# Strassen values for tiles 8 and 9, and a later place for the last two pairs of x, in a linear-attention and MLP kernel

## The chip, the cores and the metric

One core of a Trainium2 chip. The metric is the device time of one execution in microseconds, taken as the median of several runs. A profile comes from one further execution; its span runs from the first to the last instruction.

## What is computed

x is 2048 tokens by 640. Its layer norm feeds a linear attention with a learned feature map (32 heads of 20) and a GELU MLP; the attention's output, times the SiLU of the MLP's output, is added to x. Cut to what matters here:

```python
xn = _layernorm(x, axis=-1)
q, k, v = split(xn @ wqkv)                      # 32 heads of 20 each
pk = einsum("bhsd,hdf->bhsf", k, w_phi)         # pq from q alike
phi_k = concat([softmax(pk), softmax(-pk)])     # phi_q alike
kv = einsum("bhsf,bhsd->bhfd", phi_k, v)
z = einsum("bhsf->bhf", phi_k)
o = (phi_q @ kv) / (phi_q @ z + 1e-6)
s = o @ wo
g = silu(gelu(xn @ w1 + b1) @ w2 + b2)
return x + s * g
```

## The kernel before

Tokens go in 16 tiles of 128. Float32 operands are kept as a high part in the fast matmul type and a low part (value minus high part), and a product is three passes: high x high, high x low, low x high (PASSES).

**Stages.** Keys, queries and values of all tiles come first (about 0 to 238 us of the span); the MLP, and beside it the queries' normalization, follow; then the output product. The change lies in the first stage, between about 95 and 205 us. There the order on every engine is the order in which the code is written.

**A plain projection** (`project`, L392 to L404) multiplies one tile of xn by a 640x640 weight: 5 blocks x 3 passes x 2 halves, 30 matmuls of 320 columns into a `pA` bank. `pA` has three banks, taken in turn. For keys and queries `feat1` (L410 to L425) reads the bank on VectorE (`mx` L413, `e` L416, `nr` L419) and POOL adds the negative half (L420); `feat2` takes the exponential on ScalarE (L429). For keys, `key_fin` sums (L437), takes the reciprocal (L469) on VectorE and scales on POOL (L442). `kv_pair` accumulates keys times values of two tiles on TensorE (L481).

**A Strassen pair** (`token_pair`, L699 to L738) does the projection of two tiles at once with one level of Strassen's product in Winograd's form: seven groups of matmuls (QPARTS: X, Y, X, V, Z, W, Z; L714), 54 instead of 60. It needs sums of blocks of x (`x_sums`, L288; split to `xd` by `t_split`, L307 to L317) and of weights (`value_forms`, L671, split at L648 and L652). ScalarE copies X and Y (`qx`, L718, L720), POOL adds them (`qu`, L721), VectorE adds V (L725) and forms the halves (L728, L731, L735). The last group reads the bank that L728 has read. Hooks run other work between the groups. Before, values of tiles 10 to 15 and queries of tiles 8 to 15 are Strassen pairs; pair q is tiles 2q and 2q+1.

**x for a pair** comes transposed from DRAM (`load_xr`). `pair_stats` takes mean and variance of a tile's rows on VectorE (bn_stats L220), the power -0.5 on POOL (L223), and sends them through DRAM to come back spread over all partitions (`bc`, L326, L328). `pair_sub` (POOL, L335) and `pair_mul` (VectorE, L340) normalize; `plain` writes high parts (ScalarE, L272) and low parts (VectorE, L274); `x_sums` and `t_split` follow.

**The loop around the change** (L762 to L815) goes over tiles 6 to 9: key projection, features, value projection (L458 copies it), key finish, two query projections (`queries`), and between them the x work of pair t - 3. The second loop (L823 to L876) takes p = 5, 6, 7: keys of tiles 2p and 2p+1, kv of the pair before, and the value pair p with its hooks.

## Time and profile before

| | us |
|---|---|
| median of 3 runs (lowest, highest) | 639.72 (638.86, 640.79) |
| the profiled execution | 639.93 |
| its span | 638.2 |
| VectorE busy | 510.5 |
| POOL (GpSimd) busy | 432.9 |
| ScalarE busy | 260.5 |

PE is TensorE's matmuls, PEld its weight loads, DVE VectorE, ACT ScalarE, SP the engine whose queue issues most DMAs. A row of the timeline gives start, length, engine, line, operation, output and inputs; an arrow in brackets names what ended the engine's idle time ahead of it. A row of the chain gives start, length and what held the end at that time.

### The profile page before, as it was taken

The page shows a single profiled execution, that of the slowest core. Times are in us where ns is not written, and L with a number is a line of the kernel's source. Part 1 is how long each engine was busy: PE and PEld are TensorE (multiplying, and loading weights), DVE is VectorE, ACT ScalarE, POOL GpSimd, SP SyncE. Part 2 cuts the span into 40 slices and gives each one's busy share as a digit, 9 for nine tenths or more (in the row PEclk, how much of TensorE's full clock was granted, in tenths as well). Part 3 has the DMA queues.
Part 4 walks back from the last instruction along what each step waited for, and adds up shares of the span by engine and source line. Part 5 has one row for each costly group of instructions (what it writes and reads, how often), then busy time and mean ns, then how long its engine had stood idle before and what let it go on. Part 6 is the DMA issues. An engine that isn't in the chain of part 4 may idle for free.

```text
span 638.2 us, 11443 instructions
## 1 busy us (share of the span) xinstructions
PE 633.0 (99%) x4330; PEld 552.0 (86%) x4330; DVE 510.5 (80%) x784; ACT 260.5 (41%) x389; POOL 432.9 (68%) x377
## 2 busy tenths in 40 slices
PE   9999999999999999999999999999999999999997
PEld 9999999999999998888888888888888888667676
DVE  5886976789788777878989869758798899887585
ACT  3622422334344257243442534842322335455540
POOL 1877466897977764987878776381735678857363
PEclk9999999999999999999999999999999999999999
DMA  8477287394411387449899699797498598969926
GB/s 346 121 234 226 70 286 222 93 299 148 157 43 45 135 273 274 141 95 357 213 280 317 162 368 346 154 318 257 143 238 171 168 187 264 305 184 322 346 71 198
DMA packets 167167, 136.89 MB, mean 214 GB/s; under 512 B 89864, under 2 KB 130824, under 8 KB 166728
## 3 DMA queue, kind: packets, MB, share of 16 engines
q1 hardware_dynamic: 164376, 124.56, 66.0%
q10 hardware_dynamic: 2736, 11.60, 4.8%
q8 instruction: 34, 0.56, 0.4%
q14 instruction: 21, 0.17, 0.1%
HBM read 87.76 MB, written 48.38 MB: 213 GB/s over the span
## 4 chain that ended last, share of the span: by engine, by line
PE 97%; DMA 2%; DVE 0%; SPq 0%; issue 0%; DVEq 0%
PE pB L988 26%; PE pA L401 24%; PE pB L959 23%; PE pB L1190 8%; PE pA L714 6%; PE pB L1116 2%; PE pA L164 2%; PE kv L481 2%; PE qV L714 1%; DMA phT<-phi_t 1%; PE qY L714 1%; DMA xres<-in_xt_dram 1%; PE pA L545 1%; PE pB L1098 0%; PE pA L387 0%; DVE y L1199 0%
## 5 line engine op out<-in xcount | busy, mean ns | idle before, releaser
L988 PE MATMUL pB<-hs,w2s 128*128 128x512 f32 x720 | 165.9, 389 | 0.0
L988 PEld LDWEIGHTS pB<-hs,w2s 128*128 128x128 f32 x720 | 135.0, 188 | 28.8 <-issue 0.8
L959 PE MATMUL pB<-xp,w1s 128*128 128x512 f32 x324 | 81.4, 389 | 0.0
L959 PE MATMUL pB<-xd,w1s 128*128 128x512 f32 x324 | 79.3, 389 | 0.0
L442 POOL TENSOR_TENSOR eq<-eq,rc 128x1280 f32<-128x1280 f32 x16 | 37.9, 2369 | 57.3 <-DVE rc L1050 40.1
L959 PEld LDWEIGHTS pB<-xp,w1s 128*128 128x128 f32 x324 | 60.7, 188 | 12.8 <-ACT x L975 0.3
L959 PEld LDWEIGHTS pB<-xd,w1s 128*128 128x128 f32 x324 | 60.8, 188 | 12.7
L997 DVE TENSOR_TENSOR y<-pB,y 128x512 f32<-128x512 f32 x100 | 63.1, 676 | 1.8 <-PE pB L988 1.8
L964 ACT ACTIVATE pB<-pB,b1t 128x512 f32<-128x512 f32 x48 | 31.8, 662 | 77.4 <-DVE pB L1387 28.9
L429 ACT ACTIVATE e<-e 128x1280 f32<-128x1280 f32 x32 | 40.7, 1273 | 50.1 <-POOL e L420 50.1
L401 PE MATMUL pA<-wk,xp 128*128 128x320 f32 x384 | 59.6, 310 | 0.0
L401 PEld LDWEIGHTS pA<-wk,xp 128*128 128x128 f32 x384 | 56.9, 188 | 0.1
L420 POOL TENSOR_TENSOR e<-nr,e 128x640 f32<-128x640 f32 x32 | 44.7, 1396 | 17.2 <-DVE nr L419 17.2
L1037 POOL TENSOR_TENSOR ez<-eq,zrep 128x1280 f32<-128x1280 f32 x16 | 47.4, 2963 | 6.5 <-DMA eq<-e_dram 6.5
L442 POOL TENSOR_TENSOR e<-e,rc 128x1280 f32<-128x1280 f32 x16 | 37.8, 2367 | 20.4 <-DVE rc L469 20.4
L401 PE MATMUL pA<-wv,xp 128*128 128x320 f32 x240 | 37.0, 310 | 0.0
L509 POOL TENSOR_TENSOR w1s<-raw,w1s 128x640 fp32r<-128x640 f32 (+1 forms) x18 | 25.4, 1412 | 16.0 <-ACT w1s L508 15.9
L139 POOL TENSOR_TENSOR w2s<-raw,w2s 128x640 fp32r<-128x640 f32 x23 | 36.1, 1592 | 0.2 <-ACT w2s L137 0.2
L401 PEld LDWEIGHTS pA<-wv,xp 128*128 128x128 f32 x240 | 35.5, 188 | 0.1
L970 DVE TENSOR_TENSOR hs<-pB,hs 128x512 fp32r<-128x512 f32 x48 | 32.0, 684 | 4.2 <-ACT hs L966 3.8
L137 ACT ACTIVATE w2s<-raw 128x640 fp32r<-128x640 f32 x24 | 17.2, 736 | 43.1 <-DMA xd_dram<-xhi 16.4
L413 DVE TENSOR_REDUCE mx<-pA 128x32 f32<-128x640 f32 x32 | 25.9, 809 | 10.1 <-PE pA L401 9.8
(219 smaller groups left out, 1269.7 us busy)
## 6 DMA issues: line engine op xcount, KB each, us to landing
raw<-in_w_dram SPq DMA_DIRECT2D x42, 320.0 KB, 5.1
e_dram<-e ACTq DMA_DIRECT2D x16, 640.0 KB, 3.9
eq<-e_dram SPq DMA_DIRECT2D x16, 640.0 KB, 5.8
phi_t<-eq SPq DMA_DIRECT2D x64, 160.0 KB, 3.3
phT<-phi_t SPq DMA_DIRECT2D x20, 512.0 KB, 7.5
xt<-in_x_dram SPq DMA_DIRECT2D x16, 320.0 KB, 6.2
xres<-in_xt_dram SPq DMA_DIRECT2D x20, 256.0 KB, 6.7
out_dram<-xres SPq DMA_DIRECT2D x19, 256.0 KB, 4.2
```

The lines of the kernel that those rows point to most:

```text
L139: eng.tensor_tensor(sl[:, 1, :], raw, sl[:, 0, :].bitcast(F32), op=OP.subtract)
L401: nc.tensor.matmul(ps[:, hf, :HALF], stat_x(q, o, k, a), ws[k][:, b, hf * HALF:(hf + 1) * HALF], start=n == 0, stop=n == 3 * KC - 1)
L420: rest = lambda: nc.gpsimd.tensor_tensor(e5[:, :, :, 1, :], nr[:, :, :, None].to_broadcast([P, 2, 16, DH]), e5[:, :, :, 0, :], op=OP.subtract)
L429: nc.scalar.activation(ef, ef, AF.Exp)
L442: nc.gpsimd.tensor_tensor(e3, e3, rc[:, :, None].to_broadcast([P, 64, DH]), op=OP.mult)
L714: nc.tensor.matmul(bank[ch], q_x(blk, a, q), p_weight(base, f, w, k)[:, b], start=ch not in seen and n == 0, stop=n == len(mms) - 1, skip_ ...
L959: nc.tensor.matmul(bank[ch][:], tl[:, a, off + wo_:off + wo_ + P], mov(blk, b), start=new and n == 0, stop=n == len(mms) - 1, skip_group_c ...
L970: nc.vector.tensor_tensor(hs[:, 1], ps, hs[:, 0].bitcast(F32), op=OP.subtract)
L988: nc.tensor.matmul(ps[:], ws[i][:, b, d * P:(d + 1) * P], hs[o][i][:, a, :], start=i == n == 0, stop=(i, n) == (GF - 1, 2), skip_group_che ...
L997: nc.vector.tensor_tensor(y, ps[:], y, op=OP.add)
L1037: nc.gpsimd.tensor_tensor(zv, ef, zf, op=OP.mult)
L1190: nc.tensor.matmul(ps[:, mv], w, o[:, mv], start=first and n == 0, stop=last and n == len(steps) - 1, skip_group_check=True)
```

## The change

The loop over tiles 6 to 9 no longer projects the values of tiles 8 and 9. In the second loop, at p = 5, a value pair 4 stands behind the keys of tiles 10 and 11 and ahead of value pair 5, with the kv block of tiles 8 and 9 behind it; its weight sums are still split in the loop over tile 9 and in pair 4's hooks. The x work of pair 6 moves with it: `pair_sub`, `pair_mul`, `plain`, `x_sums` and `t_split` go from the loop over tile 9 into pairs 4 and 5, and `t_split` gets an engine for its second low part (VectorE for pair 6). The statistics of tiles 14 and 15 move from the loop over tile 8 into pair 4, the loads of their rows from tile 7 to tile 9, the load of pair 7 of x into pair 5. In pair 6 the kv block of tiles 10 and 11 stands behind the first group, and pair 7's high and low parts are written at two places.

```diff
--- before.py
+++ after.py
@@ -304,17 +304,13 @@
         x_sums(lambda a, b: xr[:, a:b, :P], lambda a, b: xr[:, a:b, P:],
                lambda t: xt_two(xr.rearrange("p k (o t) -> p (k o) t", o=2), t))
 
-    def t_split(q, later=False):
+    def t_split(q, eng=nc.gpsimd):
         dst = xd()[:, :, :, at(q)]
         tt = xrs.pop(q).rearrange("p k (o t) -> p (k o) t", o=2)[:, :9]
         nc.scalar.activation(dst[:, :, 0, :], tt, AF.Copy)
 
-        def lo(o):
-            nc.gpsimd.tensor_tensor(dst[:, o, 1, :], tt[:, o], dst[:, o, 0, :].bitcast(F32), op=OP.subtract)
-        lo(slice(0, 5))
-        if later:
-            return lambda: lo(slice(5, 9))
-        lo(slice(5, 9))
+        for o, e in ((slice(0, 5), nc.gpsimd), (slice(5, 9), eng)):
+            e.tensor_tensor(dst[:, o, 1, :], tt[:, o], dst[:, o, 0, :].bitcast(F32), op=OP.subtract)
 
     def pair_stats(t):
         if t % 2 == 0:
@@ -755,8 +751,8 @@
     wq_f, wq_b, wv_f = [], [], []
     queries_done = list(range(NT // 2))
     queries = iter(range(NT // 2))
-    XIN = {6: (12, 13), 7: (14, 15)}
-    STATS = {6: (10, 11), 7: (12, 13), 8: (14, 15)}
+    XIN = {6: (12, 13), 9: (14, 15)}
+    STATS = {6: (10, 11), 7: (12, 13)}
     x_in(10)
     x_in(11)
     for t in range(6, 10):
@@ -767,34 +763,36 @@
             spill(3)
         if t == 9:
             vb = value_forms(sv_raw, [nc.vector, nc.vector, nc.gpsimd, nc.gpsimd])
-            next(vb)
             w_dump(0)
             w_dump(1)
         if t == 6:
             next(vf[1])
         es[t] = feat1(pk)
-        if t == 9:
-            next(vb)
         if t > 6:
             feat2(es[t])
-            pair_mul(q)
-            pair_plain(q)
-            t_sums(q)
+            if t < 9:
+                pair_mul(q)
+                pair_plain(q)
+                t_sums(q)
         else:
             pair_sub(4)
             fold_w(wqT, range(4, KC), "wq", wq_s)
             feat2(es[t])
-        vs[t] = value(t)
-        phis[t] = key_fin(es.pop(t))
+        if t < 8:
+            vs[t] = value(t)
+        if t < 9:
+            phis[t] = key_fin(es.pop(t))
         pq = project(next(queries), wq_s)
         ef = feat1(pq)
-        if t > 6:
-            split_rest = t_split(q, t == 9)
-            if t < 9:
-                load_xr(q + 1)
+        if t == 9:
+            phis[t] = key_fin(es.pop(t))
+        if 6 < t < 9:
+            t_split(q)
+            load_xr(q + 1)
         if t == 8:
             sv_raw = [load_raw(sv_dram[k]) for k in range(4)]
         if t == 9:
+            next(vb)
             next(vb)
         for u in STATS.get(t, ()):
             pair_stats(u)
@@ -804,22 +802,34 @@
         if t == 6:
             next(vf[1])
         if t == 9:
-            next(vb)
-            next(vb)
-            next(vb)
-            split_rest()
-            load_xr(7)
-        if t in (7, 8):
-            pair_sub(q + 1)
+            for _ in range(4):
+                next(vb)
+        if t == 7:
+            pair_sub(5)
         if t < 9:
             store_e(queries_done.pop(0), ef)
-        else:
-            feat2(ef)
         if t == 6:
             kv_pair(4)
         for u in XIN.get(t, ()):
             x_in(u)
     qf, later, last_sums = None, [], []
+
+    def x_last():
+        t_split(6, nc.vector)
+        load_xr(7)
+
+    def first_store():
+        feat2(ef)
+        next(vb)
+
+    def last_stats():
+        nc.scalar.dma_start(e_dram[_tok(queries_done.pop(0))], ef)
+        pair_stats(14)
+
+    def x_mid():
+        pair_mul(6)
+        pair_stats(15)
+
     for p in range(5, 8):
         t = 2 * p
         pk = project(t, wk_s)
@@ -828,14 +838,15 @@
             qf = forms(sq_dram, wq_f, wq_b, [nc.vector, nc.vector, nc.vector, nc.gpsimd])
             next(qf)
         es[t] = feat1(pk)
+        pk = project(t + 1, wk_s)
+        if p > 6:
+            kv_pair(t - 2)
+        es[t + 1] = feat1(pk, later)
+        if p == 5:
+            value_pair(4, {1: first_store, 2: lambda: next(vb, None), 3: lambda: pair_sub(6), 4: last_stats, 6: x_mid})
+            kv_pair(8)
         if p == 6:
             pair_mul(7)
-        pk = project(t + 1, wk_s)
-        kv_pair(t - 2)
-        es[t + 1] = feat1(pk, later)
-        if p == 6:
-            plain(7, 0, xrs[7][:, :, :P])
-            plain(7, 1, xrs[7][:, :, P:], slice(0, 1))
         if p == 7:
             next(qf)
             next(qf)
@@ -845,20 +856,29 @@
 
         def rest(t=t, p=p):
             if p == 5:
-                nc.scalar.dma_start(e_dram[_tok(queries_done.pop(0))], ef)
-                next(vb)
-                next(vb, None)
+                pair_plain(6)
             later.pop(0)()
+            if p == 5:
+                t_sums(6)
+            if p == 7:
+                next(qf)
+
+        def copied(t=t, p=p):
+            feat2(es[t])
             if p == 6:
+                for o in range(2):
+                    plain(7, o, xrs[7][:, :, o * P:(o + 1) * P], lo=False)
+            if p == 7:
+                next(qf)
+
+        def x_next(p=p):
+            if p == 5:
+                x_last()
+            if p == 6:
+                plain(7, 0, xrs[7][:, :, :P], hi=False)
+                plain(7, 1, xrs[7][:, :, P:], slice(0, 1), hi=False)
                 plain(7, 1, xrs[7][:, :, P:], slice(1, 2), False, True)
                 t_sums(7)
-            if p == 7:
-                next(qf)
-
-        def copied(t=t, p=p):
-            feat2(es[t])
-            if p == 7:
-                next(qf)
 
         def first_key(t=t, p=p):
             phis[t] = key_fin(es.pop(t))
@@ -870,10 +890,12 @@
             else:
                 phis[t + 1] = es.pop(t + 1)
                 last_sums.append(key_sums(phis[t + 1]))
+            if p == 5:
+                pair_sub(7)
             if p == 6:
                 t_split(7)
 
-        value_pair(p, {0: lambda: p == 6 and plain(7, 1, xrs[7][:, :, P:], slice(1, 2), True, False), 1: rest, 2: copied, 3: lambda: p == 5 and pair_sub(7), 4: first_key, 6: second_key})
+        value_pair(p, {0: lambda: p == 6 and kv_pair(10), 1: rest, 2: copied, 4: x_next, 5: first_key, 6: second_key})
     w1f = w1_forms(w1r)
 
     def early_rest(q, ea):
```

On TensorE, in the loop over tile 9 (wk are the key weights, wv the value weights, wq the query weights, b blocks of x kept apart) stood before, from the key projection of tile 9 on:

```order
L401 MATMUL pA<-wk_185,b_1381 128x320 x6
L401 MATMUL pA<-wk_196,b_1381 128x320 x6
L401 MATMUL pA<-wk_206,xp 128x320 x6
L401 MATMUL pA<-wk_216,xp 128x320 x6
L401 MATMUL pA<-wk_240,xp 128x320 x6
L401 MATMUL pA<-wv,b_1381 128x320 x12
L401 MATMUL pA<-wv,xp 128x320 x18
L401 MATMUL pA<-wq_854,xp 128x320 x6
```

and now, at the same place:

```order
L397 MATMUL pA<-wk_185,b_1381 128x320 x6
L397 MATMUL pA<-wk_196,b_1381 128x320 x6
L397 MATMUL pA<-wk_206,xp 128x320 x6
L397 MATMUL pA<-wk_216,xp 128x320 x6
L397 MATMUL pA<-wk_240,xp 128x320 x6
L397 MATMUL pA<-wq_854,xp 128x320 x6
L397 MATMUL pA<-wq_1045,xp 128x320 x6
```

The two value rows are gone, and the query projection follows the key projection directly; the same goes for tile 8.

On VectorE, from the features of key tile 11 through pair 5, stood before (qV is the bank of group V, v the value rows, rc the sums of a key tile):

```order
L413 TENSOR_REDUCE mx<-pA 128x32
L416 TENSOR_TENSOR e<-pA,mx 128x32x20
L419 TENSOR_REDUCE nr<-e 128x32
L725 TENSOR_TENSOR qu<-qu,qV 128x320
L728 TENSOR_TENSOR v<-qu,pA 128x16x20
L437 TENSOR_REDUCE rc<-e 128x64
L469 RECIPROCAL rc<-rc 128x64
L731 TENSOR_TENSOR v<-qu,pA 128x16x20
L735 TENSOR_TENSOR v<-qu,pA 128x16x20
```

and now pair 5 stands behind the x work of pair 6:

```order
L336 TENSOR_TENSOR xr<-xr,bc 128x1280
L220 BN_STATS st<-xt 128x6 x2
L221 BN_AGGR st<-st 128x2
L222 TENSOR_SCALAR pst<-st 128x1
L225 COPY pst<-st 128x1
L274 TENSOR_TENSOR xp<-xr,xp 128x5x128
L274 TENSOR_TENSOR b_2157<-xr,b_2157 128x2x128
L274 TENSOR_TENSOR xp<-xr,xp 128x3x128
L721 TENSOR_TENSOR qu<-qu,qV 128x320
L724 TENSOR_TENSOR v<-qu,pA 128x16x20
```

The multiplication (L336), the statistics of tile 15 and three low parts (L274) of pair 6 now stand in front of pair 5's additions.

On POOL, from the sum qx of pair 5 to that of key tile 12's negative half, stood before:

```order
L721 TENSOR_TENSOR qu<-qx 128x320
L652 TENSOR_TENSOR ws<-raw,ws 128x320 x2
L420 TENSOR_TENSOR e<-nr,e 128x32x20
L335 TENSOR_TENSOR xr<-xr,bc 128x5x128 x2
L442 TENSOR_TENSOR e<-e,rc 128x1280 x2
L420 TENSOR_TENSOR e<-nr,e 128x32x20
```

and now:

```order
L717 TENSOR_TENSOR qu<-qx 128x320
L416 TENSOR_TENSOR e<-nr,e 128x32x20
L289 TENSOR_TENSOR xr<-xr 128x2x128 x4
L289 TENSOR_TENSOR xr<-xr 128x128
L313 TENSOR_TENSOR xd<-xr,xd 128x5x128
L438 TENSOR_TENSOR e<-e,rc 128x1280 x2
L331 TENSOR_TENSOR xr<-xr,bc 128x5x128 x2
L416 TENSOR_TENSOR e<-nr,e 128x32x20
```

x_sums of pair 6 (L289) and the first low part of its sums (L313) have come in between, and the mean of pair 7 (L331) stands behind the scaling of keys 10 and 11 (L438) instead of ahead of it.

More of the change, by code (lines that the diff above doesn't have):

```diff
@@ L847, in rest @@
             if p == 5:
-                nc.scalar.dma_start(e_dram[_tok(queries_done.pop(0))], ef)
-                next(vb)
-                next(vb, None)
+                pair_plain(6)
             later.pop(0)()
-            if p == 6:
-                plain(7, 1, xrs[7][:, :, P:], slice(1, 2), False, True)
-                t_sums(7)
+            if p == 5:
+                t_sums(6)
             if p == 7:
@@ L859, in copied @@
             feat2(es[t])
+            if p == 6:
+                for o in range(2):
+                    plain(7, o, xrs[7][:, :, o * P:(o + 1) * P], lo=False)
             if p == 7:
                 next(qf)
+        def x_next(p=p):
+            if p == 5:
+                x_last()
+            if p == 6:
+                plain(7, 0, xrs[7][:, :, :P], hi=False)
+                plain(7, 1, xrs[7][:, :, P:], slice(0, 1), hi=False)
+                plain(7, 1, xrs[7][:, :, P:], slice(1, 2), False, True)
+                t_sums(7)
         def first_key(t=t, p=p):
```

## The prediction

> **What bounds the kernel now.** I read the busy shares first, then who owns the chain that ended last, then that chain in order of time around the edited loop.
>
> ```profile
> PE 633.0 (99%) x4330; PEld 552.0 (86%) x4330; DVE 510.5 (80%) x784; ACT 260.5 (41%) x389; POOL 432.9 (68%) x377
> ...
> PE 97%; DMA 2%; DVE 0%; SPq 0%; issue 0%; DVEq 0%
> ```
>
> ```profile
> 119.55 39.80 PE pA L401 x270
> 159.34 1.32 PE kv L481 x125
> 160.67 1.07 PE pA L714 x6
> ...
> 168.78 8.80 PE pA L401 x60
> ```
>
> TensorE is busy for 633.0 of 638.2 us and owns 97% of the chain. The chain's pieces touch: 119.55 + 39.80 is where the kv block starts (to 0.01), 159.34 + 1.32 where pair 5 starts, and so on to the end of the loop. TensorE waits for nobody here. An edit can win only the matmuls that it takes off, and it loses every wait that it puts on TensorE; the other engines matter where they become late. One 320-column matmul costs 8.80/60 = 0.147 us, a projection of 30 costs 4.40. Pair 5 takes 168.78 - 160.67 = 8.11 us for 54 matmuls, 7.92 at that rate; its first six take 1.07 instead of 0.88, so a break in the stream costs another 0.19. I call the seven groups of a pair parts 1 to 7 (6, 6, 9, 9, 6, 9, 9 matmuls).
>
> **Term 1, the matmuls.** Values of tiles 8 and 9 were 2 x 30 matmuls and are now one pair of 54. Six less at 0.147 us: **-0.88 us**. There are as many kv blocks as before, so the breaks behind them neither grow nor fall. Nothing else leaves TensorE, so this is also the most that can be won.
>
> **Term 2, the bank of query tile 4.** Without the two value projections, query tile 6 comes to stand where key tile 9 stood, at 132.78:
>
> ```profile
> 121.29 3.15 POOL L335 TENSOR_TENSOR xr<-xr,bc 128x640 f32<-128x640 f32 x2
> 124.40 1.27 POOL L420 TENSOR_TENSOR e<-nr,e 128x640 f32<-128x640 f32 x1
> 124.47 2.55 DVE L340 TENSOR_TENSOR xr<-xr,bc 128x1280 f32<-128x1280 f32 x1 [2.60 <-POOL xr L335]
> 127.83 0.83 DVE L274 TENSOR_TENSOR xp<-xr,xp 128x640 fp32r<-128x640 f32 x1 [0.81 <-ACT xp L272]
> 129.93 1.48 DVE L437 TENSOR_REDUCE rc<-e 128x64 f32<-128x1280 f32 x1
> 131.91 0.76 DVE L413 TENSOR_REDUCE mx<-pA 128x32 f32<-128x640 f32 x1
> 132.71 0.82 DVE L416 TENSOR_TENSOR e<-pA,mx 128x640 f32<-128x640 f32 x1
> 132.78 1.92 PE L401 MATMUL pA<-wk,b 128*128 128x320 f32 x12
> ```
>
> A projection takes one of three pA banks in turn, here that of query tile 4, which VectorE frees with the subtraction L416 at 132.71 + 0.82 = 133.53. In front of that stand, unmoved by the change, POOL's subtraction for pair 5 (to 124.44), the multiplication behind it, the low parts of x and the sums of key tile 8, and none is shorter in the new order. Due at 132.78, free at 133.53: 0.75 us, and a break of 0.19 makes **+0.95** (0.75 to 1.0). A value projection of 4.40 us covered it so far. The times below go by the old clock and include this shift.
>
> **Term 3, last part of pair 5.** VectorE and POOL hold each other up when both work on SBUF operands:
>
> ```profile
> 199.64 0.96 POOL L721 TENSOR_TENSOR qu<-qx 128x320 f32<-128x320 f32 x1 [1.88 <-ACT qx L720]
> 199.95 1.01 DVE L652 TENSOR_TENSOR wqb<-raw,wqb 128x320 fp32r<-128x320 f32 x1
> 200.57 1.52 POOL L420 TENSOR_TENSOR e<-nr,e 128x640 f32<-128x640 f32 x1
> 200.88 1.56 DVE L652 TENSOR_TENSOR ws<-raw,ws 128x320 fp32r<-128x320 f32 x1
> ```
>
> They take turns. POOL's instruction ends at 200.60, VectorE's, issued in between, at 200.96; POOL's next ends at 202.09, VectorE's next at 202.44. Each VectorE subtraction of 320 columns needs some 0.36 us of its own and the rest is waiting. The Trainium skill (SBUF — State Buffer, section Who interferes with whom) calls it an exclusive lock that the first to issue holds for its whole instruction; the trace agrees (1.01 and 1.56 us for 0.36). It leaves open who is next when both have more to do. Were it always VectorE, this term would be 0.2 to 0.4, but POOL's chain in term 4 would start as late as it does now and take the difference, so the sum would move by less than 0.2.
>
> The prices:
>
> ```profile
> 103.18 1.48 DVE L340 TENSOR_TENSOR xr<-xr,bc 128x1280 f32<-128x1280 f32 x1
> 128.57 0.42 DVE L274 TENSOR_TENSOR b<-xr,b 128x256 fp32r<-128x256 f32 x1
> L274 DVE TENSOR_TENSOR xp<-xr,xp x12: 544/825/1105, 32.0 to 181.3; 128x384 fp32r<-128x384 f32 x6, 128x640 fp32r<-128x640 f32 x6
> 134.30 0.88 DVE L220 BATCH_NORM_STATS2 st<-xt 128x6 f32<-128x320 f32 x2
> 135.59 0.88 DVE L220 BATCH_NORM_STATS2 st<-xt 128x6 f32<-128x320 f32 x2
> 164.79 0.87 POOL L721 TENSOR_TENSOR qu<-qx 128x320 f32<-128x320 f32 x1
> 165.63 1.72 POOL L652 TENSOR_TENSOR ws<-raw,ws 128x320 fp32r<-128x320 f32 x2
> 165.69 0.49 DVE L725 TENSOR_TENSOR qu<-qu,qV 128x320 f32<-128x320 f32 x1 [1.24 <-POOL qu L721]
> 168.20 0.55 DVE L469 RECIPROCAL rc<-rc 128x64 f32<-128x64 f32 x1
> 185.23 3.61 POOL L289 TENSOR_TENSOR xr<-xr 128x256 f32<-128x256 f32 x5
> 188.80 4.70 POOL L442 TENSOR_TENSOR e<-e,rc 128x1280 f32<-128x1280 f32 x2
> 193.45 2.83 POOL L313 TENSOR_TENSOR xd<-xr,xd 128x640 fp32r<-128x640 f32 x2
> 188.88 1.17 ACT L310 ACTIVATE xd<-xr 128x1152 fp32r<-128x1152 f32 x1 [3.29 <-POOL xr L289]
> ```
>
> The new pair 4 I cost at nothing. It starts at 151.3; its last part, due 6.6 us later at 157.9, reads the odd half that VectorE adds in 0.49 behind part 5 (156.6), at about 157.2. But what follows is late. POOL ended the two weight subtractions (1.72) of pair 5 at 167.35 before, 6.7 us after the pair's start; in pair 4 less stands in front of them, and I take 157.0. Then come POOL's mean of pair 6 (3.15, to 160.2), VectorE's multiplication (1.48, about 161.8) and its statistics of tile 15 (135.59 - 134.30 = 1.29, about 163.1). POOL's power for them (0.5), four memsets (0.3) and the sum of the two qx of pair 5 (L721) wait in that order, so qx starts at about 164.2. At 163.8 the three low parts of x of pair 6 begin on VectorE (0.83, 0.42, 0.54 at the least). In turns: low part to 164.7, qx to 165.5, low part to 165.9, POOL's L420 of key tile 11 (1.27) to 167.1, low part to 167.6, qu + qV and the odd half (0.49 each, 0.1 between) to 168.6. Part 7 of pair 5, due at 167.4, reads that bank: **+1.45** with the break. Without turns the low parts end at 165.5 and the term is 0; if qx is first, it is 2.1.
>
> **Term 4, last part of pair 6.** From there POOL and VectorE form one chain: x_sums (3.61, its first piece free before the third low part ends; 171.0), ScalarE's high part 1.17 (172.2), VectorE's low part of four blocks 0.68 and a value half 0.49, sums and reciprocal of key 10 (1.48 + 0.55, 175.3), value half, the same of key 11 (177.7), POOL's scaling of key 11 (2.35, 180.1), its mean of pair 7 (3.15, 183.2), L420 of key 12 (1.27, 184.5), VectorE's multiplication (1.48, 186.0), qx (0.87, 186.9), two additions (188.0). The four-block low part is new on VectorE: between three blocks (0.54) and five (0.83) I take 0.68, with up to 1.6 more if POOL's five-block half goes first. Moving the kv block of keys 10 and 11 behind part 1 covers the scaling, not this. TensorE comes to part 7 of pair 6 at 185.54 - 0.88 + 0.95 + 1.45 = 187.1: **+1.1** with the break (0 to 2.5).
>
> ```profile
> 185.54 1.04 PE L714 MATMUL pA<-ws,xp 128*128 128x320 f32 x6
> 197.13 1.07 PE pA L714 x6
> ...
> core 0: us, PE busy (x) PEld busy (x) DVE busy (x) ACT busy (x) POOL busy (x), PEclk, DMA share, GB/s
> ...
> 177.00:197.00 20.00, 20.00 (x374) 19.56 (x373) 15.26 (x19) 7.75 (x11) 16.18 (x18) 1.00 0.24 67
> ...
> 196.24 1.27 POOL L420 TENSOR_TENSOR e<-nr,e 128x640 f32<-128x640 f32 x1
> 202.94 0.49 DVE L728 TENSOR_TENSOR v<-qu,pA 128x320 f32<-128x320 f32 x1
> 203.76 1.04 PE L714 MATMUL pA<-ws,xp 128*128 128x320 f32 x6
> ```
>
> The window of pairs 6 and 7 says the same in sums: POOL had 20.0 - 16.18 = 3.8 us idle there, and x_sums and mean of pair 6 bring 6.8 into this stretch while a low part (1.3) leaves.
>
> **Term 5, pair 7.** POOL's backlog (one L420, a low part, sums, two scalings, two low parts behind qx) now ends about 1.4 us after the pair starts; before, it ended at 196.24, 0.9 ahead of the pair's start at 197.13. So the L420 of keys 14 and 15 take turns with the four weight subtractions on VectorE, and the odd half, ready 0.33 early before (202.94 + 0.49 against 203.76), comes 1 us late. From 0, if the backlog is caught up, to 1.6: I take **+0.9**.
>
> **At nothing:** the statistics of tiles 14 and 15, the store of query tile 7, two dumps of wq and two loads of x rows that move. The first two leave VectorE and ACT with slack in the loop over tile 9; the dumps come out from behind the statistics on SP's queue, and the row loads have the whole of pair 4 to land. On the same queue the loads of pair 7 go out behind the statistics' round trip through DRAM, at about 170 instead of 148.45, and land 4.7 to 7.3 us later, before POOL asks at 180:
>
> ```profile
> 148.45 0.61 SPq L252 DMA_DIRECT2D xr<-in_xt_dram  x1
> DMA to landing us min/median/max: 4.7/6.0/7.3
> ```
>
> Behind pair 7 nothing changes: the query pairs leave POOL idle between groups.
>
> **Sum:** -0.88 + 0.95 + 1.45 + 1.1 + 0.9 = +3.5 us on the profiled execution's 639.93, which lies 0.2 above the median 639.72: forecast **643.2** as a median.
>
> **Rivals.** (a) Not slower: only term 2 stays, because the chain of terms 3 to 5 closes earlier than my sum; 639.72 - 0.88 + 0.95 = 639.8. It decides at part 7 of pair 6: qx there would have to be done by 184.5 instead of 186.9. For it speaks that the chain's links are single rows with starts that I worked out, against it POOL's full window. Chance 0.14. (b) The change does only what it says: 638.8; term 2 would have to vanish, though nothing in front of that L416 moves: 0.05. (c) Turns cost half and pair 7 catches up: -0.88 + 0.95 + 0.7 + 0.6 = +1.4, 641.1: 0.16. (d) Late x: the round trip takes long, the loads of pair 7 land at 181.5, 1.5 us on top: 644.7: 0.10. (e) The forecast and its neighbourhood, 641.7 to 644.4: 0.55.
>
> **Numbers.** A measurement of this kernel can tell about 0.3%, 1.9 us, from no change: 637.8 to 641.6. Faster than that is out of reach of 0.88 us: 0.02, taken from (b) for an effect outside the loop. Same is the rest of (b), (a) and nearly all of (c): 0.32. Slower is (d), (e) and a rest of (c): 0.66. The range, 639.7 to 645.2, leaves out (b), the lower part of (a) and what exceeds (d).
>
> **What would show it.** TensorE's chain should break at query tile 6 (0.8 to 1 us, waiting for VectorE's L416, L412 in the new file) and at part 7 of pairs 5, 6 and 7 (waiting for VectorE's L728, now L724), and the low parts of pair 6 (L274) should stretch beside POOL. If kv of keys 10 and 11 or part 2 of pair 7 waits instead, POOL's chain is right and its split wrong. If nothing breaks behind query tile 6, terms 3 to 5 are wrong; if nothing breaks there either, term 2 is.

## The result, and the profile after

The changed kernel takes 643.54 us (median of 6 runs, 642.79 to 645.02) where the kernel before, on the same chip, takes 639.61 (6 runs, 638.86 to 640.79). That is a ratio of 1.0059 with a 95% interval of 1.0044 to 1.0075. It is slower by 0.6%, which is 3.93 us. The forecast was 643.2. (Ratios and medians here leave out one execution, of e1_query4_first, whose granted TensorE clock was 0.655 of full speed and which took 898.72 us.) Its profiled execution takes 643.63 us with a span of 641.9; that of before had 639.93 and 638.2.

The page of the changed kernel: busy time, share and instructions of each engine (part 1), and who owns the chain that ended last (part 4):

```profile
PE 632.5 (99%) x4324; PEld 549.9 (86%) x4324; DVE 512.0 (80%) x789; ACT 259.7 (40%) x390; POOL 434.2 (68%) x377
...
PE 85%; DMA 6%; DVE 4%; POOL 3%; issue 1%; SPq 0%; ACT 0%; DVEq 0%; POOLq 0%; ACTq 0%
```

Six matmuls are gone, busy times hardly moved, and the chain is no longer TensorE's alone (97% before). What TensorE waits for, by the waits of the changed kernel (sum in us, times, longest), and below them all of its waits before, where the two rows L710 and L397 have no counterpart:

```profile
PE pA L710 <- DVE v L724: 2.4, 2, 1.2
...
PE pA L397 <- DVE e L412: 0.7, 1, 0.7
```

```profile
PE pA L545 <- PEq L1579: 0.8, 1, 0.8
PE pB L1116 <- DMA phT<-phi_t: 0.3, 1, 0.3
```

Where they stand, in TensorE's timeline of the changed kernel:

```profile
133.23 4.63 PE L397 MATMUL pA<-wq,xp 128*128 128x320 f32 x30 [0.74 <-DVE e L412]
168.37 1.14 PE L710 MATMUL pA<-ws,xp 128*128 128x320 f32 x6 [1.21 <-DVE v L724]
186.72 1.14 PE L710 MATMUL pA<-ws,xp 128*128 128x320 f32 x6
206.48 1.14 PE L710 MATMUL pA<-ws,xp 128*128 128x320 f32 x6 [1.20 <-DVE v L724]
```

These are query tile 6 and part 7 of pairs 5, 6 and 7: three of the four announced breaks are there, and that of pair 6 is not.

The part of the program that the change touches can be cut out by two TensorE rows, the kv block of tiles 6 and 7 ahead of it and the first product of the MLP behind it. I call the time between them **the stage**. First before, then after:

```profile
118.15 1.39 PE L481 MATMUL kv<-e,v 128*32 128x40 f32 x128
...
238.28 1.55 PE L959 MATMUL pB<-xp,w1s 128*128 128x512 f32 x6
```

```profile
117.71 1.39 PE L477 MATMUL kv<-e,v 128*32 128x40 f32 x128
...
241.10 1.55 PE L981 MATMUL pB<-xp,w1s 128*128 128x512 f32 x6
```

Before: 238.28 - 118.15 - 1.39 = 118.74 us. After: 241.10 - 117.71 - 1.39 = 122.00. So 3.26 of the 3.93 us lie in the stage; the other 0.67 are taken up with the last experiments. Clock times of after are 0.44 us earlier than those of before at its start (117.71 against 118.15).

### The profile page after: what moved, and what is told of

The parts are those of the page before. It is cut to its first block, busy times and chain, and to the rows that moved or that the text cites. A ratio compares the mean times of both kernels' runs of the same rounds, so it can differ in the third digit from the quotient of the medians.

```text
span 641.9 us, 11441 instructions
## 1 busy us (share of the span) xinstructions
PE 632.5 (99%) x4324; PEld 549.9 (86%) x4324; DVE 512.0 (80%) x789; ACT 259.7 (40%) x390; POOL 434.2 (68%) x377
## 4 chain that ended last, share of the span: by engine, by line
PE 85%; DMA 6%; DVE 4%; POOL 3%; issue 1%; SPq 0%; ACT 0%; DVEq 0%; POOLq 0%; ACTq 0%
PE pB L1010 25%; PE pB L981 23%; PE pA L397 14%; PE pB L1212 8%; PE pA L710 6%; PE pB L1138 2%; PE pA L164 2%; PE qV L710 1%; DMA phT<-phi_t 1%; DMA xt<-in_x_dram 1%; PE kv L477 1%; PE qY L710 1%; DMA folds<-in_wqk_dram 1%; DMA st_dram<-pst 1%; DMA xres<-in_xt_dram 1%
## 5 line engine op out<-in xcount | busy, mean ns | idle before, releaser
L438 POOL TENSOR_TENSOR eq<-eq,rc 128x1280 f32<-128x1280 f32 x16 | 37.9, 2372 | 61.1 <-DVE rc L1072 43.9
L397 PE MATMUL pA<-wk,xp 128*128 128x320 f32 x384 | 59.6, 310 | 0.0
L397 PEld LDWEIGHTS pA<-wk,xp 128*128 128x128 f32 x384 | 56.9, 188 | 0.1
L438 POOL TENSOR_TENSOR e<-e,rc 128x1280 f32<-128x1280 f32 x16 | 38.3, 2393 | 24.8 <-DVE rc L465 24.8
L397 PE MATMUL pA<-wq,xp 128*128 128x320 f32 x192 | 29.6, 310 | 0.7 <-DVE e L412 0.7
L988 ACT ACTIVATE hs<-pB 128x512 fp32r<-128x512 f32 x48 | 28.8, 600 | 2.1
```

Source lines behind the costliest of these rows:

```text
L397: nc.tensor.matmul(ps[:, hf, :HALF], stat_x(q, o, k, a), ws[k][:, b, hf * HALF:(hf + 1) * HALF], start=n == 0, stop=n == 3 * KC - 1)
L438: nc.gpsimd.tensor_tensor(e3, e3, rc[:, :, None].to_broadcast([P, 64, DH]), op=OP.mult)
```

## The experiments

Ten kernels ran: before, changed, and eight variants of the changed one (e1 to e8); three of them were profiled again (r1 to r4). The stage is worked out as above from each one's own two rows; ratios are those of the timed runs to runs of before on the same chip. A wait is the idle time in the bracket of TensorE's row; where the row has none, and for e5_three, it is the row's start less its due time (the start of the row ahead plus 0.147 us for each of its matmuls). Waits of under 0.1 us are left out.

| kernel | stage, us | ratio to before | TensorE waits in the stage, us |
|---|---|---|---|
| before (three profiles) | 118.74, 118.70, 118.70 | 1 | none |
| changed (two profiles) | 122.00, 121.96 | 1.0059 [1.0044, 1.0075] | 0.7 query tile 6; 1.2 pair 5; 1.2 pair 7 |
| e1_query4_first | 121.41 | 1.0047 [1.0030, 1.0064] | 1.3 pair 5; 0.3 pair 6; 1.2 pair 7 |
| e2_neg11_early | 120.91 | 1.0043 [1.0026, 1.0060] | 0.7 query tile 6; 0.3 pair 5; 1.2 pair 7 |
| e3_low7_vector | 120.53 | 1.0052 [1.0036, 1.0068] | 0.7 query tile 6; 1.2 pair 5 |
| e5_three | 118.85 | 1.0023 [1.0013, 1.0032] | 0.4 pair 5; 0.3 pair 6 |
| e4_stats15_late | 122.85 | one run, 644.51 us | 0.8 query tile 6; 0.8 pair 5; 1.1 pair 6; 1.2 pair 7 |
| e6_plain_values | 122.78 | 1.0087 [1.0071, 1.0102] | 0.8 query tile 6; 0.2 kv of tiles 8 and 9; 0.8 pair 5; 1.2 pair 7 |
| e7_x_in_loop | 128.58 | 1.0169 [1.0155, 1.0183] | 0.8, 0.4 query tiles 6, 7; 4.0 key tile 11; 0.8 in parts 5 and 6 and 1.2 ahead of part 7 of pair 4; 0.2 pair 7 |
| e8_five (two profiles) | 118.33, 118.33 | 1.0014 [1.0005, 1.0023] | 0.2 pair 5 |

The profiles of one kernel agree in the stage within 0.04 us. The timed ratios of e1, e2 and e3 overlap with that of the changed kernel, so what a single edit is worth is read from the stage of one profile, not from the timed runs. The times in the expectations start from 643.5 or 643.6 for the changed kernel; on the chips of the experiments before takes 639.07 (e1, e2, e3, e5) or 639.21 (e4, e6, e7, e8) instead of 639.61, so measured times come out 0.4 to 0.5 us lower for that reason alone.

### One wait at a time

**The bank of query tile 4 (term 2).** The query projection of the loop over tile 8 and its features go ahead of the x work of pair 5; that is an order of VectorE alone.

```diff
             feat2(es[t])
+            if t == 8:
+                pq = project(next(queries), wq_s)
+                ef = feat1(pq)
             if t < 9:
                 pair_mul(q)
...
-        pq = project(next(queries), wq_s)
-        ef = feat1(pq)
+        if t != 8:
+            pq = project(next(queries), wq_s)
+            ef = feat1(pq)
```

> One part alone is given back: in the loop over tile 8, query tile 4 is projected and its features (VectorE L409 to L415) are read ahead of the multiplication, the low parts of x and the key sums of tile 8. Theory: in the changed kernel TensorE waits 0.74 us ahead of query tile 6 only because the subtraction that frees the bank of query tile 4 ends at 133.1; read at 123.6 it ends at about 125.3, the due time is 132.3, so this wait and its break (0.90 together) go: 643.6 - 0.9 = 642.7. The waits of pairs 5 and 7 (1.37 and 1.36 with their breaks) stay within 0.2. Rival: VectorE is full between 124 and 142, so that what is taken from query tile 6 comes back at query tile 7 or key tile 10, and the time stays at 643.5.

The subtraction that frees the bank now ends at 125.05 + 0.82 = 125.87 (VectorE's timeline of this run), and query tile 6 waits for nothing:

```profile
125.05 0.82 DVE L412 TENSOR_TENSOR e<-pA,mx 128x640 f32<-128x640 f32 x1
```

The stage lost 0.59 us, not 0.90. The rest came back, but not where the rival had it: TensorE reaches part 7 of pair 6 earlier now than the chain that it needs. In TensorE's timeline of this run, 15 matmuls of 0.147 us from 184.07 end at 186.27; part 7 starts 0.30 later.

```profile
184.07 2.36 PE L710 MATMUL pA<-wv,xd 128*128 128x320 f32 x15
186.57 1.16 PE L710 MATMUL pA<-ws,xp 128*128 128x320 f32 x6
```

**Turns at pair 5 (term 3).** POOL's negative half of key tile 11 goes into POOL's idle time in pair 4. VectorE's order is untouched.

```diff
     def x_mid():
         pair_mul(6)
+        later.pop(0)()
         pair_stats(15)
...
             if p == 5:
                 pair_plain(6)
-            later.pop(0)()
-            if p == 5:
                 t_sums(6)
+            else:
+                later.pop(0)()
```

> One part alone: POOL's negative half of key tile 11 (L416, 1.28 us alone) leaves its place beside the low parts of x of pair 6 and runs where POOL is idle, between the powers of tiles 14 and 15 (2.33 us idle, 160.24 to 162.57). VectorE's order stays. Theory (turns of VectorE and POOL make the wait): the three low parts start at 163.45 as now and have only the sum of the two qx (to 164.2) and perhaps one piece of x_sums (0.72) to take turns with; they end at 165.7 to 166.6 instead of 167.3, the odd half at 166.9 to 167.7 against a due time of 167.0: part 7 of pair 5 waits 0 to 0.7 instead of 1.21, time 642.2 to 643.0. Rival (the order makes the wait: multiplication and statistics of tile 15 stand in front of the low parts): low parts end as late as now, wait 1.1 to 1.3, time 643.5. Pair 7's wait stays in both.

The low parts of x of pair 6 and POOL's work beside them, first in the changed kernel (timelines of VectorE and POOL), then in this run:

```profile
163.45 1.43 DVE L274 TENSOR_TENSOR xp<-xr,xp 128x640 fp32r<-128x640 f32 x1 [0.90 <-ACT xp L272]
164.81 1.50 DVE L274 TENSOR_TENSOR b<-xr,b 128x256 fp32r<-128x256 f32 x1
166.23 1.09 DVE L274 TENSOR_TENSOR xp<-xr,xp 128x384 fp32r<-128x384 f32 x1
...
167.82 0.49 DVE L724 TENSOR_TENSOR v<-qu,pA 128x320 f32<-128x320 f32 x1
...
163.33 0.88 POOL L717 TENSOR_TENSOR qu<-qx 128x320 f32<-128x320 f32 x1
164.16 1.86 POOL L416 TENSOR_TENSOR e<-nr,e 128x640 f32<-128x640 f32 x1
165.98 3.97 POOL L289 TENSOR_TENSOR xr<-xr 128x256 f32<-128x256 f32 x5
```

```profile
163.48 1.42 DVE L274 TENSOR_TENSOR xp<-xr,xp 128x640 fp32r<-128x640 f32 x1 [0.91 <-ACT xp L272]
164.82 0.41 DVE L274 TENSOR_TENSOR b<-xr,b 128x256 fp32r<-128x256 f32 x1
165.16 1.09 DVE L274 TENSOR_TENSOR xp<-xr,xp 128x384 fp32r<-128x384 f32 x1
...
166.75 0.49 DVE L724 TENSOR_TENSOR v<-qu,pA 128x320 f32<-128x320 f32 x1
...
165.04 3.86 POOL L289 TENSOR_TENSOR xr<-xr 128x256 f32<-128x256 f32 x5 [0.83 <-DVE xp L274]
```

The same three subtractions run in the same order, and the first two start when they did. Only the one in the middle has lost its neighbour on POOL, and it takes 0.41 us instead of 1.50. The other two still stand beside the sum of the qx and the first piece of x_sums and take as long as before. The odd half (L724) comes 1.07 us earlier, part 7 of pair 5 starts 0.28 behind its due time, and the stage is 1.09 us shorter. The order alone, the rival, would have left the wait where it was. What is left, 0.28, is within the 0 to 0.7 that was expected.

**What stands in front of the low parts.** The complement: POOL's turns stay, and the statistics of tile 15 leave their place in front of the low parts.

```diff
     def x_mid():
         pair_mul(6)
-        pair_stats(15)
...
             if p == 5:
+                pair_stats(15)
                 x_last()
```

> From the changed kernel, the statistics of tile 15 alone (VectorE, 161.18 to 162.5; POOL's power for them) leave their place between the multiplication and the low parts of x of pair 6 and run behind the odd half of pair 5, where VectorE is idle (168.3 to 171.2). Theory (the low parts are late because ScalarE's high part, behind the two qx copies, is ready only at 163.4, and because of POOL's turns; the queue in front of them is no cause): they start at 163.45 as now, only the qx sum on POOL may start 0.3 to 0.5 earlier; part 7 of pair 5 waits 0.8 to 1.3 (now 1.21). Rival (what stands in front of the low parts sets the wait): they start 1.3 earlier and the wait is gone. The mean of pair 7 on POOL (now 179.05) does not wait for the later round trip in either.

The first low part, in VectorE's timeline of this run:

```profile
163.78 1.05 DVE L274 TENSOR_TENSOR xp<-xr,xp 128x640 fp32r<-128x640 f32 x1 [2.19 <-ACT xp L272]
```

This run's clock is 0.31 us later than the changed kernel's (its kv block starts at 118.02, not 117.71), so the low part starts when it did. It still waits for ScalarE, the turns are there, and part 7 of pair 5 waits 0.83, within what was expected. What I had put down as harmless was not. Behind the statistics SP issues the loads of pair 7 of x, and these are now late; POOL's mean of pair 7 waits for them, and part 7 of pair 6 for 1.05 us. In POOL's timeline of this run, and on SP's queue in this run and in the changed kernel:

```profile
180.25 3.13 POOL L331 TENSOR_TENSOR xr<-xr,bc 128x640 f32<-128x640 f32 x2 [1.21 <-DMA xr<-in_xt_dram]
```

```profile
174.25 0.52 SPq L253 DMA_DIRECT2D xr<-in_xt_dram  x1
```

```profile
167.28 0.52 SPq L253 DMA_DIRECT2D xr<-in_xt_dram  x1
```

From the second load's issue to POOL's start are 180.25 - 174.25 = 6.0 us. In the changed kernel it goes out at 167.28; if it takes as long there, it has landed at about 173.3, 5.8 us before POOL asks at 179.05. That is an estimate from this one load. Rival (d) of the prediction is a real mechanism with a margin of some 6 us.

**Turns at pair 7 (term 5).** One word: the second low part of the sums of pair 7 moves from POOL to VectorE.

```diff
-                t_split(7)
+                t_split(7, nc.vector)
```

> One word alone: the second low part of the sums of x of pair 7 (four blocks, 1.4 us on POOL) goes to VectorE, as the change does for pair 6. Theory (pair 7 waits because POOL's backlog of 1.4 us makes its negative halves of keys 14 and 15 and the qx sum take turns with VectorE's four weight subtractions): POOL is through 1.4 earlier, the first two weight subtractions take 1.6 to 2.0 instead of 3.27 and the odd half is there before 205.12: wait of part 7 of pair 7 from 1.20 to 0 to 0.3, time 642.3 to 642.6. VectorE has 1.41 idle behind key tile 14 that takes the 0.7 (or 1.5 with a turn). Rival (the high parts on ScalarE, L644, or VectorE's own queue set these subtractions): the wait stays 1.0 to 1.2 or moves to key tile 15, time 643.4 or more.

The first two weight subtractions, in VectorE's timelines of the changed kernel and of this run:

```profile
199.59 3.27 DVE L648 TENSOR_TENSOR ws<-raw,ws 128x640 fp32r<-128x640 f32 x2
```

```profile
200.34 1.60 DVE L648 TENSOR_TENSOR ws<-raw,ws 128x640 fp32r<-128x640 f32 x2
```

They take 1.60 us instead of 3.27 and the wait at pair 7 is gone; the stage is 1.47 us shorter, where 643.6 to between 642.3 and 642.6 had meant 1.0 to 1.3. The timed median, 642.39, is 3.32 over before on its chip, where the changed kernel is 3.93 over: it shows 0.6 of it, and the last experiments take up why. The added low part took 1.64 us on VectorE instead of 0.7, in turn with POOL's scaling, and fell into idle time.

### Are the three waits independent?

> The three edits of the other runs of this set together. If the three waits were independent: 643.6 - 0.9 - 1.0 - 1.3 = 640.4. Theory: TensorE then reaches part 7 of pair 6 some 1.9 to 2.3 earlier, while the chain of POOL and VectorE that ends there just in time now (odd half at 186.67, TensorE there at 186.70) comes only 1.4 to 1.6 earlier; a new wait of 0.3 to 0.9 with its break stands at part 7 of pair 6, time 640.7 to 641.3. Rival 1: the waits are independent and nothing new comes: 640.4. Rival 2 (the three waits are one and the same lateness that moves on): over 642.

The edit is the three diffs above together. Alone they shortened the stage by 0.59 + 1.09 + 1.47 = 3.15; together by 122.00 - 118.85 = 3.15. By size that is rival 1 (3.2), and more than the theory allowed (643.6 - 640.7 = 2.9 at most). By place the theory is right: part 7 of pair 6 is late. Both hold, because that lateness had come with the first edit alone (0.30 in e1_query4_first) and does not grow. Its chain can be read in this run's chain of waits:

```profile
177.85 3.17 POOL xr L331 x2
...
182.50 1.86 POOL qu L717
184.36 0.02 issue
184.39 0.50 DVE qu L721
...
184.98 0.50 DVE v L724
185.48 0.04 issue
185.52 1.58 PE pA L710 x9
```

From the mean of pair 7 to the sum of the qx POOL holds the end, then VectorE's two additions, then part 7 of pair 6, 0.31 us behind its due time. At pair 5 another 0.37 is left. The timed median, 640.34, is 1.27 over before on its chip; of this only 118.85 - 118.74 = 0.11 is in the stage, so it cannot choose between the theory and rival 1.

### The pair, or the move?

**The pair undone.** Two plain value projections stand at the place of pair 4.

```diff
-            value_pair(4, {1: first_store, 2: lambda: next(vb, None), 3: lambda: pair_sub(6), 4: last_stats, 6: x_mid})
+            first_store()
+            next(vb, None)
+            vs[8] = value(8)
+            pair_sub(6)
+            last_stats()
+            vs[9] = value(9)
+            x_mid()
```

> From the changed kernel, Strassen's product alone is undone: the values of tiles 8 and 9 are two plain projections at the place of pair 4 (60 matmuls instead of 54), with the moved x work around them as it is now. Theory (the pair itself brings its six matmuls, 0.88 us, and costs nothing; the loss is lost cover and turns): TensorE reaches pair 5 about 0.8 later, the waits at query tile 6 (0.74) and pair 7 (1.2) stay, that at pair 5 stays within 0.4 (its low parts hang on ScalarE's copies of pair 5's own products, which move along): 644.2 to 644.6 where the changed kernel has 643.5, 1.0070 of before. Rival (the pair's additions, copies and memsets are what makes the engines late): the waits of pairs 5 and 7 go, 642 or less, 1.003 of before.

Two pieces of the value weights already hold the pairs' sums at this place, so the values of tiles 8 and 9 are of other weights here; the instructions are those of a plain projection. The stage is 0.78 us longer than the changed kernel's (six matmuls are 0.88), and all three waits are still there, so the rival is out. The total, 644.46, lies in the expected range, the ratio, 1.0087, above the expected 1.0070. Strassen's product brings about what its matmuls say. That it costs nothing is shown only for the balance: without it the wait at pair 5 is 0.39 us shorter (0.82 for 1.21), and one of 0.16 at the kv block of tiles 8 and 9 is new.

**The move undone.** Pair 4 stays, and the x work of pair 6 with the statistics of tiles 14 and 15 returns to the loop.

```diff
-    XIN = {6: (12, 13), 9: (14, 15)}
-    STATS = {6: (10, 11), 7: (12, 13)}
+    XIN = {6: (12, 13), 7: (14, 15)}
+    STATS = {6: (10, 11), 7: (12, 13), 8: (14, 15)}
...
-            if t < 9:
-                pair_mul(q)
-                pair_plain(q)
-                t_sums(q)
+            pair_mul(q)
+            pair_plain(q)
+            t_sums(q)
...
-        if 6 < t < 9:
+        if t > 6:
             t_split(q)
             load_xr(q + 1)
...
-        if t == 7:
-            pair_sub(5)
+        if t in (7, 8):
+            pair_sub(q + 1)
```

(and the same calls leave pairs 4 and 5).

> From the changed kernel, the move alone is undone: pair 4 stays behind the keys of tiles 10 and 11, but the x work of pair 6 and the statistics of tiles 14 and 15 stand in the loop over tiles 8 and 9 again, as before. Theory (the move costs what it costs at pairs 5 to 7, but it is the smaller evil, because VectorE has no room in the loop without the value projections): TensorE waits 0.9 at query tile 6 as now, some 0.4 more at query tile 7 behind the statistics, 1.5 to 2.2 at key tile 11 (query tile 6 is read behind multiplication and low parts of pair 6) and 0.5 to 1.5 at pair 4; the wait of pair 5 is gone, that of pair 7 stays or shrinks to 0.5: 643.5 to 646, 1.006 to 1.010 of before. Rival (the moved x work is the whole loss, the loop has room): only query tile 6 waits, 640.0, 1.0005 of before.

The theory has the side right: the loop without its two value projections has no room for this work, and the stage is 9.84 us longer than before. The waits at the query tiles and at pairs 5 and 7 are as expected; pair 4 has 2.0 where 0.5 to 1.5 was expected. But the size is missed, 649.89 us where at most 646 was expected, above all for two reasons. First, key tile 11 waits 4.03 us instead of 1.5 to 2.2: POOL's mean of pair 6 held up the multiplication, which ends at 146.81, and the bank of query tile 6 is freed at 151.47 (VectorE's timeline of this run):

```profile
144.26 2.55 DVE L336 TENSOR_TENSOR xr<-xr,bc 128x1280 f32<-128x1280 f32 x1 [2.48 <-POOL xr L331]
...
150.65 0.82 DVE L412 TENSOR_TENSOR e<-pA,mx 128x640 f32<-128x640 f32 x1
```

Second, key tile 11 itself then takes 158.36 - 151.63 = 6.73 us instead of 4.40. The reason stands in the last section.

### What was left, and the rest of the span

The kernel with five edits adds two to the three: ScalarE writes the first high part of x of pair 6 ahead of pair 5's copies, and the sums of key tile 10 run while VectorE waits for the high part of the sums.

```diff
         pair_mul(6)
+        plain(6, 0, xrs[6][:, :, :P], lo=False)
         later.pop(0)()
...
-                pair_plain(6)
+                plain(6, 0, xrs[6][:, :, :P], hi=False)
+                plain(6, 1, xrs[6][:, :, P:])
...
             if p == 5:
+                phis[t] = key_fin(es.pop(t))
                 x_last()
```

(`first_key` leaves key tile 10 out at p = 5.)

> The three edits that worked, and two more against what was left (0.37 at part 7 of pair 5, 0.31 at part 7 of pair 6): ScalarE writes the first high part of x of pair 6 right behind the multiplication, ahead of pair 5's copies, so that the first low part starts at about 162.0 instead of 162.97; and the sums of key tile 10 run on VectorE while it waits for the high part of the sums of pair 6 (166.8 to 169.7 idle), so that POOL scales key tile 10 there and its chain towards pair 6 ends some 2 us earlier. Theory: both waits go, and the stage from query tile 4 to the MLP is 0.88 - 0.25 = 0.6 shorter than before, 0.999 of before (638.4 where before has 639.1). Rival: POOL's earlier scaling takes turns with the low part of the sums and with x_sums and the wait at pair 6 stays (0.2 to 0.5), 1.000 of before or a little over.

Both waits went: the low parts of x of pair 6 start at 162.06 and take 0.81, 0.42 and 0.55 us, without a turn. 0.16 us for a copy on ScalarE, which now comes behind the early high part, took their place. TensorE's waits in this run, all of them (the first two lie outside the stage):

```profile
PE pA L541 <- PEq L1610: 0.8, 1, 0.8
PE pB L1147 <- DMA phT<-phi_t: 0.3, 1, 0.3
PE pA L710 <- ACT qx L714: 0.2, 1, 0.2
```

The stage is 118.74 - 118.33 = 0.41 us shorter than before (expected 0.6), the best of all, and yet the timed runs give 640.19 against 639.21, 1.0014 [1.0005, 1.0023], where 0.999 was expected. It beats the changed kernel and not the one before. Four further profiles ask whether the rest of the span is the reason.

> The kernel before, profiled once more. From the end of the kv block of tiles 6 and 7 to the first product of the MLP (the stage of the change) the first profile has 118.74 us (119.54 to 238.28), the rest of its span 519.5. Open is why the two repaired kernels, whose stages are 118.85 and 118.33, still ran 1.0023 and 1.0014 of before. Theory: the rest of the span scatters by half a microsecond and more (loads of x rows and of transposed queries near the end), the stage does not: stage 118.7 to 118.8, rest 518.6 to 519.5. Rival: the rest is steady in each kernel and longer in the changed ones.

> The kernel before a third time, for the scatter. Theory: stage 118.7 to 118.8 again, rest anywhere from 518.6 to 519.6. Rival: rest within 0.1 of the other two profiles of before.

> The changed kernel once more: its first profile has 122.00 in the stage and 519.9 in the rest. Theory: stage 121.9 to 122.1 with the same three waits (0.74, 1.21, 1.20), rest 518.8 to 520.2, overlapping with before. Rival: rest 519.9 to 520.2, above every profile of before.

> The kernel with five edits once more: its first profile has 118.33 in the stage and 520.1 in the rest. Theory: stage 118.3 to 118.4, rest 518.8 to 520.2, overlapping with before. Rival: rest 520.0 to 520.2, above every profile of before, so that something outside the stage costs the changed kernels half a microsecond.

Rest of the span (span minus stage): before 519.46, 520.00 and 519.10; changed 519.90 and 518.84; five edits 520.07 and 519.37. The stage repeats within 0.04 us and the rest scatters by 0.7 to 1.1 us in each kernel, so it isn't steady, and the kernels overlap. That is the theory's side, though the 520.00 of r1_before lies outside its 518.6 to 519.5.

The timed runs are on the rival's side. Take from each kernel's median that of before on its chip, and then the difference of the stages. The changed kernel has 0.67 us left, e1 0.46, e2 0.71, e3 1.53, e5 1.16, e6 1.21, e7 0.84 and e8 1.39. If the stage is as steady in the timed runs as in the profiles, the rest is longer than before's in all eight. A part can be seen at the end of the profiles: from the end of the last product by TensorE's timeline to the end of the span are 4.09, 4.30 and 4.19 us in the three of before and 4.28 to 4.95 in the eleven others. Why the kernels differ there, where their code is the same, and where the other part lies, stays open.

## Why the prediction was right

In time it was right, in part by luck; it was right in three of its four waits by place and by the main cause. By its terms, each against the changed kernel's timeline:

| term | forecast, us | measured, us |
|---|---|---|
| 1, six matmuls | -0.88 | -0.88 by count; 0.78 when undone |
| 2, query tile 6 | +0.95 | +0.90 |
| 3, pair 5 | +1.45 | +1.37 |
| 4, pair 6 | +1.1 | +0.02 |
| 5, pair 7 | +0.9 | +1.36 |
| sum | +3.5 | +2.8, stage +3.26 |

The measured terms are a part's start less its due time. The due times come from these rows of TensorE's timeline:

```profile
129.69 2.80 PE L397 MATMUL pA<-wk,xp 128*128 128x320 f32 x18
...
164.80 2.36 PE L710 MATMUL pA<-wv,xd 128*128 128x320 f32 x15
...
184.50 2.36 PE L710 MATMUL pA<-wv,xd 128*128 128x320 f32 x15
...
202.92 2.36 PE L710 MATMUL pA<-wv,xd 128*128 128x320 f32 x15
```

Query tile 6 was due at 129.69 + 18 x 0.147 = 132.33 and started at 133.23. Part 7 of pair 5 was due at 164.80 + 15 x 0.147 = 167.00 and started at 168.37; likewise 186.70 against 186.72 and 205.12 against 206.48. The 0.5 us of the stage that the terms don't hold are small breaks of about 0.1 each, at part 2 of pair 7, at the kv blocks, and behind each wait, where the due time does not see them.

**Term 2** is right in place, cause and size: read earlier, the bank makes no wait (e1_query4_first).

**Term 3** is right in place and in its main cause, shown from both sides: take POOL's neighbour away and the wait shrinks by its price (e2_neg11_early), take the queue in front away and the low parts start no earlier (e4_stats15_late). The prediction gave their start as 163.8 on before's clock, 163.36 on this one (0.44 less); it is 163.45. In front of them it named only VectorE's own queue, the statistics. In fact ScalarE's high part, behind the copies of pair 5, held them; it ended at 163.42, the statistics at 162.55.

```profile
162.69 0.73 ACT L272 ACTIVATE xp<-xr 128x640 fp32r<-128x640 f32 x1
```

The size owes something to luck too. POOL's sum of the qx came first (163.33 against 163.45), the order for which the prediction gave 2.1, not 1.45. It came 0.43 earlier than forecast (164.2 - 0.44 = 163.76), and that makes up for more than half of the difference to the measured 1.37.

**Term 4** is the one that was mis-sized, +1.1 against nothing. The mechanism is there, with no slack: the second addition ended at 186.18 + 0.49 = 186.67 and TensorE came at 186.70.

```profile
186.18 0.49 DVE L724 TENSOR_TENSOR v<-qu,pA 128x320 f32<-128x320 f32 x1
```

On this clock the forecast had 187.56 and 186.66. So TensorE's arrival was right and the chain 0.89 too long. Of that, 0.6 is x_sums: I had it end at 170.56, it ended at 165.98 + 3.97 = 169.95, since POOL's first piece started beside the second low part and ran ahead of the third, 1.0 earlier than forecast, and the pieces then took 0.4 longer. The other 0.3 is the end of the chain. I laid POOL's L420 of key 12, VectorE's multiplication and the sum of the qx one behind the other, but the multiplication waits only for the mean and takes turns with both. That the chain nevertheless ends just in time was seen when TensorE came earlier: then part 7 of pair 6 waits 0.30 (e1_query4_first) and 0.31 (e5_three).

**Term 5** is right in cause (e3_low7_vector) and 0.46 too small. The backlog was well placed: it ended at 196.73 + 2.80 = 199.53, 1.2 us behind the pair's start at 198.33, forecast 1.4. The turns were priced too low: the two subtractions of 640 columns took 3.27 where e3_low7_vector has 1.60, and behind them the two of 320 columns still met POOL.

**At nothing** held for pair 4, the statistics, the stores and the loads. Rival (a) fell with terms 3 and 5, but at part 7 of pair 6, which the prediction named as the place that decides, it was (a) that held. (b) fell with term 2, (c) because turns cost in full, (d) by a margin of some 5.8 us. That terms 4 and 5 erred in opposite directions helped. So did 0.5 us of small breaks and 0.67 us outside the stage, for which the prediction has no term and without which the measured terms give 2.8 of the 3.93 us. 643.54 against 643.2 is closer than the terms deserve.

## What to carry to other kernels

Work that leaves a stage is also cover that leaves it: look which bank or buffer is now asked for earlier and who stands in front of its reader. Work that VectorE and POOL both do on SBUF operands should be priced as turns, and a single instruction moved from the turns into idle time, or handed to the other engine, can be worth a microsecond of its stage while every busy time hardly moves. Of several small waits remove all, but expect a chain that ended just in time to be the next. And compare the whole time as well as the stage: here the repaired stage was 0.41 us shorter than before and the whole time 1.0 us longer.

## What the runs showed of the hardware that I had not expected

In e7_x_in_loop TensorE waited 4.03 us ahead of key tile 11, and its clock went down. The projection in TensorE's timeline, and the granted clock (1.00 or 0.50, the third figure from the end, ahead of DMA share and GB/s) in windows of 1 us of that run:

```profile
151.63 3.54 PE L397 MATMUL pA<-wk,b 128*128 128x320 f32 x12 [4.03 <-DVE e L412]
154.96 3.56 PE L397 MATMUL pA<-wk,xp 128*128 128x320 f32 x18
```

```profile
147.00:148.00 1.00, 0.60 (x5) 0.33 (x3) 0.33 (x1) 1.00 (x3) 0.00 (x0) 1.00 1.07 215
...
149.00:150.00 1.00, 0.00 (x0) 0.00 (x0) 1.00 (x2) 0.00 (x0) 0.92 (x2) 0.91 1.05 342
150.00:151.00 1.00, 0.00 (x0) 0.00 (x0) 0.91 (x2) 0.00 (x0) 0.92 (x2) 0.50 1.11 340
...
156.00:157.00 1.00, 1.00 (x6) 1.00 (x6) 0.97 (x2) 1.00 (x3) 1.00 (x1) 0.67 0.77 323
157.00:158.00 1.00, 1.00 (x9) 1.00 (x8) 1.00 (x2) 0.28 (x1) 1.00 (x2) 1.00 0.81 333
```

TensorE was busy for 0.60 us of the window that starts at 147, so it stopped at 147.6. The mean of 0.91 in the window from 149 puts the fall to 0.50 at about 149.8, and the mean of 0.67 from 156 the return at about 156.7, 5 us into the work. The first twelve matmuls take 154.96 - 151.63 = 3.33 us, 0.28 each instead of 0.147. So the wait of 4.03 us cost another 2.33 in the projection behind it. The waits of 0.7 to 1.2 us in the changed kernel left the clock at 1.00.

The Trainium skill (TensorE: Matmul & The Clock Gate, Part 1: The HAM clock gate) gives half the clock after an idle window of about 3.4 us and the full clock after about as much sustained work. The halving agrees. Here the clock fell after some 2.2 us of idleness and took 5 us to return; for the fall this run is shorter than the page says, and the run decides.
